# Token weight kept in its own column order, first keys and queries transposed apart, third transposes moved two steps forward

## The chip, the cores and the metric

The kernel runs on one core of a Trainium2 chip. The metric is device time in microseconds (us) of one execution, lower is better. Where a difference is small, kernels are compared within rounds on one chip. The engines have short names: PE is TensorE (matmuls), PEld its weight loads, ACT is ScalarE, DVE is VectorE, POOL is GpSimd. SBUF and PSUM are the two memories in which the kernel keeps its tiles; its matmuls write to PSUM. A *span* is the length that the trace covers; it is about 1.8 us less than the time (374.2 against 376.01 in the kernel before).

## The reference

A squared-ReLU attention without softmax feeds a two-stage mixer: first a product over tokens with a residual, then a product over channels with a residual.

```python
# q, k, v: 8 x 12 x 448 x 64, float32
scores = q @ k.T / sqrt(64)
attn   = maximum(scores, 0)**2 / 448
x      = heads_joined(attn @ v)                       # 8 x 448 x 768
h      = maximum(x.T @ w_tok1, 0) @ w_tok2            # tokens 448 -> 256 -> 448
u      = x + h.T
out    = u + maximum(u @ w_ch1, 0) @ w_ch2            # channels 768 -> 1536 -> 768
```

## The kernel before

Work goes in *groups* of four heads: 24 groups, of which three make one batch entry. Each group takes seven *steps*; a step makes the scores of 64 keys on PE, the ReLU on ACT, the square on DVE, and later the product with the values on PE. The mixer's products of earlier groups are put between the steps. The order on each engine is that of the program; nothing is rescheduled.

The kernel divides its PSUM into slots: two slots `att` (scores), one each of `acc0` and `acc1`, and two slots `bank`. A tile that takes a slot waits until the last tile there has been read: in the trace of the kernel before, PE stood 0.49 us ahead of the first token matmuls, until DVE had copied `qkT` out of the `bank` slots.

Tokens are loaded as `(p c)`, token = 7p + c, so that every load is contiguous. Inside the kernel tokens are kept as `(c p)`. The second token weight, whose columns are tokens, therefore has to be put into `(c p)` order: GpSimd does that with two copies.

```python
def load_wt2():
    nc.gpsimd.dma_start(out=wt2_nat, in_=moe_w_tok2.rearrange("(c j) s -> j c s", c=JC))

def order_wt2():
    for j in range(JC):                                   # JC = 2
        nc.gpsimd.tensor_copy(
            wt2[:, j, :].rearrange("n (c p) -> n c p", c=QC),
            wt2_nat[:, j, :].rearrange("n (p c) -> n c p", c=QC))

def transposes(i, place="acc", split=False):
    # ... 56 transposing matmuls: queries and keys of group i into two PSUM slots
    for r in range(2):                                    # then one copy of each, 128x896
        (nc.scalar.copy if split and r == 0 else nc.vector.tensor_copy)(
            sb[:, r].rearrange("n w t -> n (w t)"), parts[r][:, : 2 * S])

def x_back(i, place="bank", copy=None):
    # ... 8 transposing matmuls into a tile x_ps in `place`, then one copy to x_sb

def token2(i, ...):
    # ... h_ps = r1^T @ wt2, two matmuls for each r
        nc.vector.tensor_tensor(                          # the residual addition
            out=uT_tiles[b // 2][:, 2 * d + r, off : off + S],
            in0=parts[r][:, :S], in1=xT[b % 2][:, 2 * d + r, :S], op=ALU.add)
```

The opening, before PE's queue is full of mixer work, is written out by hand. Its `keep_clock` matmuls of zeros were put there with the intent of keeping PE's clock up.

```python
load_four(0, "kqv"); load_four(1, "qk"); load_wt1(); load_four(2, "qk")
load_four(1, "v");   load_wt2();         load_four(2, "v"); load_four(3, "qk")
order_wt2()
load_wc1(0, 2);      load_four(3, "v")
keep_clock(2, warm_ps)                       # matmuls of zeros
transposes(0, "acc", split=True)
keep_clock(3, warm_ps)
for i in range(DB):                          # groups 0, 1, 2
    for c in range(QC):                      # 7 steps
        scores(i, c, alone=(i, c) == (0, 2))
        if i == 0:
            keep_clock(0 if c in (3, 4) else 1 if c > 4 else 2, warm_ps)
        # ...
        square(keep=1)
        # ... values of group i-1 at c < 3, token2(i-2) at c = 1, 2
        if c == 4 and i > 0:
            x_back(i - 1, place="acc0", copy=nc.scalar.copy if i > 1 else None)
        if c == 5 and i > 0:
            transposes(i + 1, "bank")
        if c == 6:
            values(i, (0, 1))                # opens acc0 and acc1
            if i > 0:
                token1(i - 1)                # the first token matmuls
```

## Time and profile before

| | us |
|---|---|
| time, median of 3 | 376.94 (376.81 to 377.26) |
| PE busy, in a span of 374.2 | 365.0 |
| residual additions on DVE, 48 | 27.7 |

The prediction below shows the head of the page, the stretches and the chain. Three more lines of the timeline of the kernel before serve as marks for everything that follows (columns: start, length, engine, line, operation, tiles; in brackets the idle time before it and what ended it): the first scores, the first token matmuls, and the first use of the reordered weight.

```profile
7.74 0.38 PE L172 MATMUL sc_ps<-qkT 64*64 64x448 bf16 x4 [0.36 <-ACT qkT L162]
...
20.00 1.03 PE L276 MATMUL t_ps<-x_sb,wt 128*128 128x256 bf16 x8 [0.49 <-DVE qkT L162]
...
22.23 0.55 PE L335 MATMUL h_ps<-wt,r_sb 128*128 128x448 bf16 x2
```

From the group of residual additions (mean ns of one after the bar):

```profile
L345 DVE TENSOR_TENSOR uT_sb<-h_ps,xT 128x448 bf16<-128x448 f32 x48 | 27.7, 617 | 9.3 <-PE h_ps L335 9.3
```

### The profile page before, as it was taken

The page shows a single profiled execution, that of the slowest core. Times are in us where ns is not written, and L with a number is a line of the kernel's source. Part 1 is how long each engine was busy: PE and PEld are TensorE (multiplying, and loading weights), DVE is VectorE, ACT ScalarE, POOL GpSimd, SP SyncE. Part 2 cuts the span into 40 slices and gives each one's busy share as a digit, 9 for nine tenths or more (in the row PEclk, how much of TensorE's full clock was granted, in tenths as well). Part 3 has the DMA queues.
Part 4 walks back from the last instruction along what each step waited for, and adds up shares of the span by engine and source line. Part 5 has one row for each costly group of instructions (what it writes and reads, how often), then busy time and mean ns, then how long its engine had stood idle before and what let it go on. Part 6 is the DMA issues. An engine that isn't in the chain of part 4 may idle for free.

```text
span 374.2 us, 10241 instructions
## 1 busy us (share of the span) xinstructions
PE 365.0 (98%) x4379; PEld 201.8 (54%) x4379; DVE 213.1 (57%) x413; ACT 211.5 (57%) x313; POOL 101.2 (27%) x187
## 2 busy tenths in 40 slices
PE   8889999999999999999999999999999999999996
PEld 3544555455555555565555555555555654555554
DVE  2996688756576666475555684575555755131022
ACT  4987888776345368725765457752775456312400
POOL 8975448304221403430330303412310000000000
PEclk9999999999999999999999999999999999999999
DMA  8999999923997876766755677757560434233024
GB/s 153 126 141 202 181 206 185 170 44 66 141 169 166 168 133 99 114 108 151 108 92 92 112 142 132 111 77 159 112 95 13 99 81 98 58 70 86 0 54 116
DMA packets 69565, 43.32 MB, mean 116 GB/s; under 512 B 43472, under 2 KB 66064, under 8 KB 69520
## 3 DMA queue, kind: packets, MB, share of 16 engines
q0 software_dynamic: 24496, 21.49, 40.3%
q1 hardware_dynamic: 44640, 20.75, 25.6%
q8 instruction: 34, 0.56, 0.6%
q10 hardware_dynamic: 384, 0.43, 0.4%
q14 instruction: 11, 0.09, 0.1%
HBM read 43.42 MB, written 11.01 MB: 145 GB/s over the span
## 4 chain that ended last, share of the span: by engine, by line
PE 90%; DVE 5%; ACT 3%; issue 1%; DVEq 0%; ACTq 0%
PE m_ps L425 29%; PE m_ps L386 28%; PE sc_ps L172 9%; PE acc_ps L205 9%; PE h_ps L335 4%; PE t_ps L294 3%; PE qkT_ps L148 3%; ACT at L186 2%; DVE at L193 2%; PE t_ps L310 1%; DVE uT_sb L345 1%; PE t_ps L276 1%; PE warm_ps L521 1%; DVE qkT L162 1%; PE x_ps L258 1%
## 5 line engine op out<-in xcount | busy, mean ns | idle before, releaser
L186 ACT ACTIVATE at<-sc_ps 128x896 bf16<-128x896 f32 x167 | 144.9, 924 | 48.6 <-PE sc_ps L172 48.5
L193 DVE TENSOR_TENSOR at<-at 128x896 bf16<-128x896 bf16 x168 | 99.2, 628 | 54.5 <-ACT at L186 54.4
L386 PE MATMUL m_ps<-uT_sb,wc 128*128 128x448 bf16 x564 | 115.5, 353 | 0.2 <-DVE uT_sb L345 0.2
L425 PE MATMUL m_ps<-wc,r_sb 128*128 128x384 bf16 x660 | 113.2, 326 | 0.0
L425 PEld LDWEIGHTS <-r_sb 128*128 128x128 bf16 x660 | 62.7, 98 | 46.7 <-issue 6.1
L393 ACT ACTIVATE r_sb<-m_ps 128x448 bf16<-128x448 f32 x94 | 51.3, 546 | 56.0 <-PE m_ps L386 55.6
L386 PEld LDWEIGHTS <-wc 128*128 128x128 bf16 x564 | 52.3, 98 | 53.4 <-issue 8.3
L432 DVE TENSOR_TENSOR out_sb<-m_ps,u_sb 128x384 f32<-128x384 f32 x55 | 30.6, 556 | 48.3 <-PE m_ps L425 46.8
L172 PE MATMUL sc_ps<-qkT 64*64 64x448 bf16 x672 | 54.1, 358 | 1.0 <-ACT at L186 0.6
L223 DVE TENSOR_SCALAR xT<-acc_ps 128x448 bf16<-128x448 f32 x45 | 26.1, 620 | 27.6 <-PE acc_ps L205 27.6
L205 PE MATMUL acc_ps<-at,v_raw 64*64 64x448 bf16 x672 | 41.0, 350 | 0.8 <-ACT x_sb L267 0.5
L642 POOL COPY gate<-x_sb 1x1 bf16<-1x1 bf16 x12 | 3.1, 261 | 126.6 <-DMA x_sb<-xT 126.6
L84 POOL DMA_DIRECT2D q_raw<-in_q_dram x48 | 28.9, 613 | 18.7 <-DMA wc<-in_moe_w_ch_dram 16.3
L345 DVE TENSOR_TENSOR uT_sb<-h_ps,xT 128x448 bf16<-128x448 f32 x48 | 27.7, 617 | 9.3 <-PE h_ps L335 9.3
L84 POOL DMA_DIRECT2D v_raw<-in_v_dram x48 | 29.6, 643 | 5.9 <-DMA wc<-in_moe_w_ch_dram 4.5
L320 ACT ACTIVATE r_sb<-t_ps 128x256 bf16<-128x256 f32 x36 | 11.8, 381 | 32.5 <-PE t_ps L310 28.3
L162 DVE COPY qkT<-qkT_ps 128x896 bf16<-128x896 bf16 x45 | 26.0, 619 | 6.7 <-PE qkT_ps L148 6.7
L205 PEld LDWEIGHTS <-v_raw 64*64 64x64 bf16 x672 | 21.9, 106 | 14.6 <-issue 4.8
L172 PEld LDWEIGHTS <-qkT 64*64 64x64 bf16 x672 | 17.5, 105 | 21.7 <-issue 17.8
L84 POOL DMA_DIRECT2D k_raw<-in_k_dram x46 | 28.1, 633 | 1.7 <-issue 1.7
L335 PE MATMUL h_ps<-wt,r_sb 128*128 128x448 bf16 x96 | 22.3, 353 | 0.0
L294 PE MATMUL t_ps<-x_sb,wt 128*128 128x256 bf16 x108 | 14.7, 273 | 0.0
(53 smaller groups left out, 153.1 us busy)
## 6 DMA issues: line engine op xcount, KB each, us to landing
out_dram<-out_sb SPq DMA_DIRECT2D x54, 192.0 KB, 3.1
q_raw<-in_q_dram POOLq DMA_DIRECT2D x48, 112.0 KB, 4.0
v_raw<-in_v_dram POOLq DMA_DIRECT2D x48, 112.0 KB, 5.3
k_raw<-in_k_dram POOLq DMA_DIRECT2D x46, 112.0 KB, 4.5
wc<-in_moe_w_ch_dram POOLq DMA_DIRECT2D x4, 1152.0 KB, 10.6
u_sb<-uT_sb SPq DMA_TRANSPOSE x48, 2.6
x_sb<-xT SPq DMA_TRANSPOSE x16, 3.3
k_first<-in_k_dram SPq DMA_DIRECT2D x1, 224.0 KB, 3.5
```

The source lines that it names most:

```text
L84: eng.dma_start(out=dst[64 * r : 64 * (r + 1)].rearrange("p g c d -> p g (c d)"), in_=src[b, h0 : h0 + 2].rearrange("g (p c) d -> p g (c d ...
L162: (nc.scalar.copy if split and r == 0 else nc.vector.tensor_copy)(sb[:, r].rearrange("n w t -> n (w t)"), parts[r][:, : 2 * S])
L172: nc.tensor.matmul(ps[64 * r : 64 * (r + 1), g, :S], lhsT=sb[h, r, 1, c * 64 : (c + 1) * 64], rhs=sb[h, r, 0, :], start=True, stop=True, s ...
L186: nc.scalar.activation(at, ps[:, :, :S], AF.Relu)
L193: nc.vector.tensor_tensor(out=at, in0=at, in1=at, op=ALU.mult)
L205: nc.tensor.matmul(ps[r][64 * g : 64 * (g + 1), :S], lhsT=v_raw[h, g, c, :], rhs=at[h, g, :], start=(c == 0), stop=(c == QC - 1), skip_gro ...
L335: nc.tensor.matmul(parts[r][:, :S], lhsT=r1[:, j, r * 128 : (r + 1) * 128], rhs=wt2[:, j, :], start=(j == 0), stop=(j == JC - 1),)
L345: nc.vector.tensor_tensor(out=uT_tiles[b // 2][:, 2 * d + r, off : off + S], in0=parts[r][:, :S], in1=xT[b % 2][:, 2 * d + r, :S], op=ALU.add,
L386: nc.tensor.matmul(ps[:, :S], lhsT=wc1[:, g, e * 128 : (e + 1) * 128], rhs=uT[:, g, off : off + S], start=(g == 0), stop=(g == CC - 1),)
L393: nc.scalar.activation(r2[:, e, off : off + S], ps[:, :S], AF.Relu)
L425: nc.tensor.matmul(ps[:, :HN], lhsT=r2[:, e, t * 128 : (t + 1) * 128], rhs=wc2[:, e, cols], start=(e == 0), stop=(e == EC - 1),)
L432: nc.vector.tensor_tensor(out=o[:, cols].rearrange("n (g d) -> n g d", d=128), in0=ps[:, :HN].rearrange("n (g d) -> n g d", d=128), in1=u_ ...
```

## The change

The intent is a shorter opening: take GpSimd's copies out of the way by reading the PSUM result in permuted order instead; let the first scores start sooner; and bring the third transposes (group 2) forward, so that their copies do not stand between `x_sb` and the first token matmuls. Five parts: (1) no reordering, (2) the permuted read, (3) the first keys and queries apart, (4) one pair of clock-keeping matmuls fewer, (5) the move.

```diff
-            out=wt2_nat, in_=moe_w_tok2.rearrange("(c j) s -> j c s", c=JC)
+            out=wt2, in_=moe_w_tok2.rearrange("(c j) s -> j c s", c=JC)
-    def order_wt2(): ...                                  # and its call
+    def transposes_first():
+        keys = [ps_acc.tile([128, 1024], BF16, tag=f"acc{r}", name="kT_ps") for r in range(2)]
+        queries = ps_att.tile([128, 2, 1024], BF16, tag="att", name="qT_ps")
+        # ... 28 transposes of the keys, then
+                nc.scalar.copy(sb[:, 0, 1], keys[0][:, :S])
+                nc.vector.tensor_copy(sb[:, 1, 1], keys[1][:, :S])
+        # ... 28 transposes of the queries, then
+                nc.vector.tensor_copy(sb[:, :, 0], queries[:, :, :S])
@@ the residual addition
-                out=uT_tiles[b // 2][:, 2 * d + r, off : off + S],
-                in0=parts[r][:, :S],
-                in1=xT[b % 2][:, 2 * d + r, :S],
+                out=uT_tiles[b // 2][:, 2 * d + r, off : off + S].rearrange("n (c p) -> n c p", c=QC),
+                in0=parts[r][:, :S].rearrange("n (p c) -> n c p", c=QC),
+                in1=xT[b % 2][:, 2 * d + r, :S].rearrange("n (c p) -> n c p", c=QC),
@@ the opening
-    transposes(0, "acc", split=True)
+    transposes_first()
-                keep_clock(0 if c in (3, 4) else 1 if c > 4 else 2, warm_ps)
+                keep_clock(2 if c < 3 else c // 6, warm_ps)
-            if c == 5 and i > 0:
+            if (i, c) in ((1, 3), (2, 5)):
                 transposes(i + 1, "bank")
```

More of the change, by code (lines that the diff above doesn't have):

```diff
@@ L64 @@
     wt1_last = wpool.tile([128, 128], BF16, name="wt1_last")
-    wt2_nat = wpool.tile([128, JC, S], BF16, name="wt2_nat")
     wt2 = wpool.tile([128, JC, S], BF16, name="wt2")
@@ L105, in load_wt2 @@
         nc.gpsimd.dma_start(
-            out=wt2_nat, in_=moe_w_tok2.rearrange("(c j) s -> j c s", c=JC)
+            out=wt2, in_=moe_w_tok2.rearrange("(c j) s -> j c s", c=JC)
         )
-    def order_wt2():
-        for j in range(JC):
-            nc.gpsimd.tensor_copy(
-                wt2[:, j, :].rearrange("n (c p) -> n c p", c=QC),
-                wt2_nat[:, j, :].rearrange("n (p c) -> n c p", c=QC),
-            )
     def load_wc1(i, parts):
@@ L164, in transposes @@
             )
+    def transposes_first():
+        sb = attn.tile([128, 2, 2, S], BF16, name="qkT")
+        qkT[0] = sb
+        keys = [ps_acc.tile([128, 1024], BF16, tag=f"acc{r}", name="kT_ps") for r in range(2)]
+        queries = ps_att.tile([128, 2, 1024], BF16, tag="att", name="qT_ps")
+        for w, dst in ((1, keys), (0, [queries[:, r] for r in range(2)])):
+            for c in range(QC):
+                for r in range(2):
+                    h = slice(64 * r, 64 * (r + 1))
+                    for g in range(2):
+                        nc.tensor.matmul(
+                            dst[r][64 * g : 64 * (g + 1), c * 64 : c * 64 + 64],
+                            lhsT=raws[0, "qk"[w]][h, g, c, :],
+                            rhs=ident[h, h],
+                            is_transpose=True,
+                            start=True,
+                            stop=True,
+                            skip_group_check=True,
+                        )
+            if w:
+                nc.scalar.copy(sb[:, 0, 1], keys[0][:, :S])
+                nc.vector.tensor_copy(sb[:, 1, 1], keys[1][:, :S])
+            else:
+                nc.vector.tensor_copy(sb[:, :, 0], queries[:, :, :S])
     def scores(i, c, alone=False):
@@ L544 @@
     load_four(3, "qk")
-    order_wt2()
     load_wc1(0, 2)
```

## The prediction

> **What bounds the kernel now.** I read the head of the profile page first, then busy time by stretch, then the chain of waits, and last the timeline of the stretch that was not full.
>
> From the page (busy time by engine, then busy tenths in 40 slices of 9.36 us):
>
> ```profile
> PE 365.0 (98%) x4379; PEld 201.8 (54%) x4379; DVE 213.1 (57%) x413; ACT 211.5 (57%) x313; POOL 101.2 (27%) x187
> ...
> PE   8889999999999999999999999999999999999996
> ```
>
> TensorE is busy 98% of the span, and only the first three slices and the last fall short. The table of stretches gives PE 10.00 of 10 us in 40 to 50, 50.00 of 50 in 80 to 130, and 100.00 of 100 in 200 to 300. So from about 38 us to 370 us a shorter operation elsewhere buys nothing, and a longer one costs nothing until PE has to wait for it. The change removes no useful matmul. All it can win is PE's gaps in the first 38 us, and once that opening is shorter, the full stretch behind it moves forward by as much. The stretches of the opening (columns: window, length, busy us of PE, PEld, DVE, ACT, POOL):
>
> ```profile
> 5.00:10.00 5.00, 4.64 (x95) 2.37 (x97) 1.90 (x4) 3.19 (x4) 4.45 (x10) 1.00 1.22 176
> 10.00:15.00 5.00, 4.17 (x116) 2.85 (x117) 5.00 (x10) 4.55 (x6) 5.00 (x9) 1.00 0.79 90
> 15.00:20.00 5.00, 3.99 (x102) 2.36 (x97) 4.59 (x10) 5.00 (x7) 3.36 (x6) 1.00 1.20 176
> 20.00:25.00 5.00, 4.46 (x52) 2.01 (x51) 5.00 (x8) 3.98 (x7) 4.77 (x7) 1.00 0.70 91
> 25.00:30.00 5.00, 4.48 (x113) 2.80 (x114) 4.49 (x9) 4.41 (x7) 2.31 (x4) 1.00 1.15 206
> ```
>
> PE's gaps from 5 to 30 us are 0.36+0.83+1.01+0.54+0.52 = 3.3 us; the bound there is DVE or ACT, each in turn at 5.00 of 5.00. The chain of waits says which, and when (columns: start us, duration us, what):
>
> ```profile
> 16.81 0.82 ACT at L186
> 17.63 0.02 issue
> 17.65 0.62 DVE at L193
> 18.28 0.60 DVE x_sb L267
> 18.88 0.53 DVE at L193
> 19.41 1.07 DVE qkT L162 x2
> 20.48 2.06 DVE at L193 x2
> 22.54 0.22 issue
> 22.76 0.61 DVE at L193
> 23.37 0.55 DVE uT_sb L345
> 23.92 0.04 issue
> 23.96 0.20 ACT xT L219
> ```
>
> ACT leads up to 17.6 us, then DVE from 17.65 to 23.9, then ACT. The "20.48 2.06" step is odd: two squares in 2.06 us, where the two copies before them took 1.07.
>
> [...] The square reads `at` from SBUF twice; GpSimd's reordering of the second token weight reads SBUF. [...] Timeline of the stretch:
>
> ```profile
> 20.23 2.12 POOL L111 COPY wt<-wt_nat 128x448 bf16<-128x448 bf16 x2 [1.87 <-DMA wt_nat<-in_moe_w_tok_dram]
> 20.39 2.98 DVE L193 TENSOR_TENSOR at<-at 128x896 bf16<-128x896 bf16 x3
> ```
>
> and the squares' durations (ns min/median/max), in 20.2 to 23.5 us, then in 12.7 to 16.3:
>
> ```profile
> L193 DVE TENSOR_TENSOR at<-at x3: 611/1203/1319, 20.4 to 22.8; 128x896 bf16<-128x896 bf16 x3
> L193 DVE TENSOR_TENSOR at<-at x6: 619/622/627, 12.8 to 15.6; 128x896 bf16<-128x896 bf16 x6
> ```
>
> Two squares lost 1203+1319-2x622 = 1278 ns while the two GpSimd copies ran.
>
> [...] The kernel before has no VectorE read of PSUM at a 28-byte step, so the trace decides nothing.
>
> **The change part by part.**
>
> 1. Reordering of the second token weight removed. POOL loses two copies (880 and 1294 ns) and the 1.87 us it waited for their input. DVE gets 1.28 us back, on the chain. POOL reaches the load of half the first channel weight at about 18.4 instead of 22.3 us, which fills a hole in which the DMA engines stood at a share of 0.19 and 0.16 (22 to 24 us). Nobody waits for that load: it landed at 22.3+9.2 = 31.5 and was first used at 33.4.
>
> 2. Permuted read in 48 residual additions: the same 448 elements at 617 ns each; only the PSUM operand's inner step grows from 4 to 28 bytes. If free: 0. [...]
>
> 3. First keys and queries apart. Before, the last transpose let both copies start at 6.8; ACT's 896 elements took 0.91 us and PE's scores waited for it until 7.73. Afterwards the key copies (448 elements[...]) run beside the query transposes, and one DVE copy of 2x448 (0.62, as the old DVE copy of 896) starts at about 6.85 and ends at 7.45. Scores 0.24 us earlier. The six clock-keeping matmuls end at 7.37, so they don't hold it.
>
> 4. One clock-keeping pair fewer (at c=5 of the first group). Before, PE waited 0.67 us at 12.40 for a DVE copy because that pair needed a bank. ACT ran without a gap from 10.38 to 16.38, so this wait was just tied; removing it is what lets part 3's 0.24 us through. Alone: about 0.
>
> 5. Third transposes (group 2) two steps earlier: PE work and the two DVE copies (1.07 us) move from after the fifth score step to after the third. DVE had 0.36 us idle before 17.65; the copies start near 17.0 and use it. More important, the first token matmul waited at 20.0 for those copies to free its banks; now it needs only `x_sb`, which I place at 19.25. ACT's next result, at(2,0), comes at about 20.8 instead of 21.56. The risk is the data: the second half of those keys was issued at 12.3 and landed 4.1 us later, at 16.4, and the transposes would now ask for it at about 16.1. Estimate: PE stands 0.3 us, just covered because ACT is the bound until 17.4.
>
> Sum: the gains overlap, since parts 1 and 5 relieve the same DVE chain (17.65 to 23.4) and then ACT's own chain limits. ACT restarts at 20.3 instead of 21.07 and runs nearly gapless to 26.9, so about 0.8 us passes (0.24 of it part 3), while DVE's further relief (the first residual addition at 22.2 instead of 23.3) is partly slack. I choose 0.8 to 1.3 us, 1.0 as the middle, if the permuted read is free.
>
> **Rivals.**
>
> A. The permuted read is slow. [...] I give it 30%.
>
> B. The moved transposes wait for their keys: [...]the next scores wait too and ACT starves. For: 16.4 against 16.1. Against: only 0.3 us. If the load were 1 us later, half the gain goes: 376.5.
>
> C. The opening is held by something later anyway (data of group 4, or the channel weight's landing), so the shift is absorbed by about 37 us. Against: groups 3 and 4 were landed 2 us or more before use, and part 1 only moves loads forward. Time: 376.9.
>
> D. GpSimd's copies hid in the chain (DVE just waits for ACT instead). Partly built in above: that is why I count 1.0, not 1.9.
>
> **Range and chances.** [...]the free case is the likelier, so I name 376.1, a little above its centre of 375.9. Low 375.0: all of parts 1, 3 and 5 (1.28+0.24+0.36 = 1.9) pass. High 377.7: rival A nearly whole. A 2% change is 7.5 us, more than twice all the gaps in 5 to 30 us[...]: within 2% is all but certain.
>
> **What would show it.** Right: the residual addition stays at about 617 ns; no GpSimd copy of the weight, and no square over 0.7 us near 20 to 22 us; scores start near 7.5; the first token matmul near 19.3 with no wait for `qkT`; the steady stage still 100% PE, the whole shifted by about 1 us. Wrong: [...]PE waiting for `k_raw` near 16 us and ACT idle after it (B); the same steps up to 37 us and then a wait for a load (C). A slower clock in the opening, from the pair of clock-keepers that is gone, would be a cause that I have not counted.

Marks in the prediction, and in the expectations further down, stand for passages that were cut because no trace or run of this case shows what they say. The forecast's sum came to 376.5 us: 0.7 of the free case (376.94-1.0) and 0.3 of the case of a slow permuted read. The terms of the slow case, an extra time for each addition and what it would add on the path, are cut, and that weighing with them; the 376.1 that was named and the upper end of 377.7 were chosen with them in view. The estimate for part 3's key copies is cut too; in the trace after they took 532 ns on ACT and 391 ns on DVE.

## The result, and the profile after

Ratios here and below are the mean time of one kernel's fast runs over that of the other's fast runs of the same rounds, so not quite the ratio of the medians that are quoted; the brackets are 95% intervals.

| | median us | runs |
|---|---|---|
| before | 376.91 | 4 (376.81 to 377.26) |
| changed | 376.38 | 4 (376.01 to 376.56) |
| ratio | 0.9983 | [0.9966, 1.0] |

The times differ by 0.53 us: the same by the 2% measure, with an interval that reaches 1.0, and about two thirds of the 0.84 us that were predicted. The head of the page after, and its group of residual additions:

```profile
PE 365.0 (97%) x4377; PEld 201.2 (54%) x4377; DVE 212.1 (57%) x414; ACT 211.0 (56%) x313; POOL 99.1 (26%) x185
...
PE   7889999999999999999999999999999999999996
...
L363 DVE TENSOR_TENSOR uT_sb<-h_ps,xT 128x448 bf16<-128x448 f32 x48 | 27.7, 616 | 9.4 <-PE h_ps L353 9.3
```

The permuted addition took 616 ns, where the plain one took 617. The row of tenths differs in the first digit alone, and there PE is less busy than before, not more. The stretches of the opening after (window, length, busy us of PE, PEld, DVE, ACT, POOL, then clock, DMA share, GB/s):

```profile
5.00:10.00 5.00, 3.92 (x90) 2.14 (x87) 2.00 (x5) 2.64 (x4) 4.25 (x9) 1.00 1.17 170
...
20.00:25.00 5.00, 4.67 (x60) 1.93 (x52) 3.52 (x8) 3.88 (x7) 2.35 (x4) 1.00 1.20 195
```

The clock is 1.00 in all five stretches from 5 to 30 us. Below, *the lock* is what the prediction reads from the trace: two of DVE's squares took 1203 and 1319 ns while GpSimd's copies ran, against 622 ns for the middle one of the six squares in 12.7 to 16.3 us. By what mechanism was not shown. DVE in 20 to 25 us fell from 5.00 to 3.52, as the removal of the lock should make it, yet PE gained only 0.21 there. In 5 to 10 us PE lost 0.72. The chain of waits after (start, length, what) says why:

```profile
2.15 4.70 DMA q_raw<-in_q_dram
...
7.35 0.64 DVE qkT L182
...
8.03 0.41 PE sc_ps L190 x4
...
17.44 1.07 DVE qkT L154 x2
...
19.04 0.61 DVE x_sb L285
```

In this execution the first queries landed 4.70 us after their issue, at 6.84, and the first scores started at 8.03, 0.29 *later* than before. ACT, which was to restart at 20.3 (21.07 before), did so at 21.29. At the other end the copies of the third transposes (`qkT` L154) are now ahead of `x_sb`, which ends at 19.65. The timeline after, from there:

```profile
19.70 0.57 PE L223 MATMUL acc_ps<-at,v_raw 64*64 64x448 bf16 x8 [0.72 <-DVE x_sb L285]
20.20 1.05 PE L294 MATMUL t_ps<-x_sb,wt 128*128 128x256 bf16 x8
...
22.72 0.62 DVE L211 TENSOR_TENSOR at<-at 128x896 bf16<-128x896 bf16 x1 [1.48 <-ACT at L204]
```

PE no longer waits for `qkT` before the first token matmuls (second line, no bracket), as predicted. But it waits 0.72 us just ahead of them (first line). And DVE, freed of the lock, stands 1.48 us for ACT (third line). The first residual addition, predicted at 22.2, came at 23.27; before it came at 23.30. One more time is close: the second token weight, issued at 14.56, landed 7.8 us later, at about 22.4, and PE used it from 22.44. The change takes the copies away, not the dependence on when that load lands.

Measured from the first scores, the first token matmuls came after 12.26 us before and 12.17 us after. So two questions are open: where the 0.53 us come from, if the opening is hardly shorter in these two traces, and why the move brought nothing. The second has a candidate in the first line above. For the first, a single pair of traces is not enough: the profiled execution of the kernel before took 376.01 us, well under its median.

### The profile page after: what moved, and what is told of

Same layout as the page of the kernel before. It is cut to its first block, busy times and chain, and to the rows that moved or that the text cites. A ratio compares the mean times of both kernels' runs of the same rounds, so it can differ in the third digit from the quotient of the medians.

```text
span 374.7 us, 10236 instructions
## 1 busy us (share of the span) xinstructions
PE 365.0 (97%) x4377; PEld 201.2 (54%) x4377; DVE 212.1 (57%) x414; ACT 211.0 (56%) x313; POOL 99.1 (26%) x185
## 4 chain that ended last, share of the span: by engine, by line
PE 89%; DVE 6%; ACT 1%; DMA 1%; issue 1%; POOL 0%; ACTq 0%; POOLq 0%; DVEq 0%
PE m_ps L443 29%; PE m_ps L404 28%; PE acc_ps L223 9%; PE sc_ps L190 9%; PE h_ps L353 4%; PE t_ps L312 3%; DVE at L211 2%; PE qkT_ps L140 2%; PE t_ps L294 1%; DMA q_raw<-in_q_dram 1%; DVE uT_sb L363 1%; PE t_ps L328 1%; ACT at L204 1%; DVE qkT L154 1%; PE x_ps L276 1%
## 5 line engine op out<-in xcount | busy, mean ns | idle before, releaser
L211 DVE TENSOR_TENSOR at<-at 128x896 bf16<-128x896 bf16 x168 | 97.7, 619 | 55.9 <-ACT at L204 55.9
L190 PE MATMUL sc_ps<-qkT 64*64 64x448 bf16 x672 | 53.2, 358 | 1.1 <-ACT at L204 0.9
L241 DVE TENSOR_SCALAR xT<-acc_ps 128x448 bf16<-128x448 f32 x45 | 26.1, 620 | 27.6 <-PE acc_ps L223 27.6
L83 POOL DMA_DIRECT2D q_raw<-in_q_dram x48 | 28.9, 614 | 19.9 <-DMA wc<-in_moe_w_ch_dram 17.4
L223 PEld LDWEIGHTS <-v_raw 64*64 64x64 bf16 x672 | 21.4, 106 | 15.7 <-issue 5.7
L154 DVE COPY qkT<-qkT_ps 128x896 bf16<-128x896 bf16 x44 | 25.3, 616 | 5.4 <-PE qkT_ps L140 5.4
```

Of the source, the lines that this page charges most:

```text
L83: eng.dma_start(out=dst[64 * r : 64 * (r + 1)].rearrange("p g c d -> p g (c d)"), in_=src[b, h0 : h0 + 2].rearrange("g (p c) d -> p g (c d ...
L190: nc.tensor.matmul(ps[64 * r : 64 * (r + 1), g, :S], lhsT=sb[h, r, 1, c * 64 : (c + 1) * 64], rhs=sb[h, r, 0, :], start=True, stop=True, s ...
L211: nc.vector.tensor_tensor(out=at, in0=at, in1=at, op=ALU.mult)
L223: nc.tensor.matmul(ps[r][64 * g : 64 * (g + 1), :S], lhsT=v_raw[h, g, c, :], rhs=at[h, g, :], start=(c == 0), stop=(c == QC - 1), skip_gro ...
```

## The experiments

All outputs were correct. Medians, counts and ranges are of timed runs. *Opening* is the time from the first scores to the start of the fifth group's 56 transposes, both as the chain of waits of the profiled execution has them; *weight wait* is what PE waited for the reordered weight there. Kernels with the same letter ran on the same chip.

| kernel | | median us (range, runs) | ratio to before | first scores | opening | weight wait |
|---|---|---|---|---|---|---|
| before, first trace | | | | 7.74 | 30.08 | 0 |
| changed, first trace | | | | 8.03 | 29.99 | none |
| before_again | A | 376.54 (376.03 to 377.37, 5) | 0.9995 [0.9981, 1.0009] | 7.64 | 30.64 | 0.46 |
| after_again | A | 376.2 (376.01 to 377.99, 6) | 0.9991 [0.9974, 1.0008] | 7.38 | 30.96 | none |
| only_weight | A | 376.41 (375.88 to 376.51, 5) | 0.9986 [0.9972, 1.0] | 7.63 | 30.07 | none |
| xback_first | A | 376.03 (375.87 to 378.74, 6) | 0.9992 [0.997, 1.0015] | 7.67 | 30.38 | none |
| only_first | B | 376.49 (376.26 to 377.5, 6) | 0.9998 [0.9981, 1.0014] | 7.48 | 31.50 | 1.27 |
| reorder_twice | B | 378.99 (378.65 to 380.27, 6) | 1.0066 [1.0048, 1.0084] | 8.05 | 33.69 | 2.56 |
| qk2_early | B | 376.1 (375.91 to 376.29, 6) | 0.998 [0.9965, 0.9994] | 7.69 | 29.99 | none |
| qk2_early_xback | B | 375.74 (375.25 to 376.12, 6) | 0.997 [0.9956, 0.9985] | 7.62 | 29.45 | none |
| lock_kept | C | 376.48 (376.02 to 376.89, 6) | 0.9995 [0.9981, 1.0009] | 7.57 | 30.20 | none |
| weight_first | C | 375.76 (375.61 to 375.99, 5) | 0.9974 [0.9961, 0.9988] | 7.64 | 29.88 | none |
| after_third | C | 375.99 (375.77 to 376.93, 6) | 0.9984 [0.9969, 0.9998] | 7.36 | 30.10 | none |
| best_again | C | 375.47 (375.05 to 376.0, 6) | 0.9967 [0.9953, 0.998] | 7.77 | 29.46 | none |

What follows the opening, that is the span less the start of the fifth group's transposes, was 336.36 to 336.95 us in all fourteen traces, with the plain and with the permuted addition, and no kernel stands apart in it. So what is larger than this spread happens before that point, and a single trace carries a spread of some 0.3 us to either side from the rest alone. Where an effect is smaller than that, the timed runs decide, or nothing does.

**Theory and rivals, after the first comparison.** Theory: the gain comes from part 1, through the lock as predicted, and part 5 gains nothing because a new wait (the slot `acc0`) took the old one's place. Rival 1: the gain of part 1 is not the lock but the time at which the weight is ready. Rival 2: part 5 fails because the moved transposes wait for their keys. Rival 3: the gain is from part 3, and part 1 is off the path. In the expectations the lock (the 1.28 us that the squares lost) is Theory B, Rival 1 is Theory D, Rival 2 Theory C and Rival 3 Theory A; in xback_first and reorder_twice "Theory A" means the claim in its own brackets.

### The two kernels again, and the weight's parts alone

The kernel before and the changed one ran again, unedited (before_again, after_again, and later after_third). only_weight is the kernel before with parts 1 and 2 alone.

> The kernel before against itself: the noise floor. Ratio 1.000 within 0.001. In the trace, if the first queries land 0.6 us later than in the first trace, the first scores start at about 8.3 instead of 7.74 us, and the whole is longer by as much; the stretch from first scores to the first transposes after the opening stays at 30.1 us.

> The changed kernel again, timed in more rounds. Theory A (the first keys and queries apart bring nearly all of the gain, some 0.27 us, the rest is near nothing): 0.3 to 0.6 us under the kernel before. Theory B ([...]1.28 us of squares): 0.8 us or more. In the trace: residual addition 0.616 us; how late the first queries land decides when the first scores start, 7.5 us if they land by 6.3, about 8.0 if at 6.84 as in the first trace.

> The changed kernel once more, beside the others on this chip: 376.0 to 376.5 us, without a group at 377. In its trace the second token matmuls wait for no weight.

> Only the second token weight in natural order with the permuted read (no GpSimd copy); the rest as before. Theory A: no gain, 0 to 0.2 us, because ScalarE waits for the first token matmul's result at about 20 to 21 us whatever the squares cost, and is gapless after it; squares at 0.62 us, and VectorE now idles near 21 to 22.5 us for about 1 us. Theory B: 0.6 to 1.2 us faster.

In the repeated kernel before, the ratio was as expected, but its opening did not stay at 30.1 us. Over all rounds the kernel before ran 42 times, mean 376.78, spread from 375.95 to 378.11 us. Cut at 376.8, a line that was drawn after the times were seen and that no clean gap marks, 20 runs lie below (mean 376.38) and 22 above (mean 377.14). The changed kernel ran 16 times, mean 376.33, and only 2 of the 16 are above 376.8. So its mean is that of the lower part of the kernel before: the upper part is what is nearly missing. In two of the three comparisons within rounds the interval reaches or includes 1.0 (0.9983, 0.9991, 0.9984), so the size of the gain is not known well. The second trace of the kernel before (time 376.84) shows what the upper part may be:

```profile
20.43 2.47 POOL L111 COPY wt<-wt_nat 128x448 bf16<-128x448 bf16 x2 [2.17 <-DMA wt_nat<-in_moe_w_tok_dram]
...
22.95 0.35 PE L335 MATMUL h_ps<-wt,r_sb 128*128 128x448 bf16 x1 [0.46 <-POOL wt L111]
```

The weight landed 0.2 us later than in the first trace, the copies took 2.47 us instead of 2.12, and PE stood 0.46 us for the second half of the weight. The opening was 0.56 us longer.

only_weight (0.9986) has as large a gain as the changed kernel, by itself: by the ratio about 0.5 us, more than the 0.2 us at most of Theory A and less than the 0.6 us of Theory B. Its trace shows what the theory's lock is worth. The timeline, at the place of the removed wait:

```profile
22.12 0.55 PE L327 MATMUL h_ps<-wt,r_sb 128*128 128x448 bf16 x2
...
22.40 0.62 DVE L185 TENSOR_TENSOR at<-at 128x896 bf16<-128x896 bf16 x1 [0.96 <-ACT at L178]
```

DVE has its 1.28 us back and idles 0.96 us of them for ACT. The opening is 30.07 us, against 30.08 in the trace of the kernel before in which the weight was in time. In that comparison the lock was worth nothing. The kernel before shows why: the third square, at 22.76 us, needs a result that ACT began at 21.56 and took 0.91 us for, so without the lock it could have started about 0.3 us earlier at most. By the value matmuls near 27 us, which wait for ACT's copy of `x_sb`, even that is gone: they started 19.37 us after the first scores in both traces.

### The lock without the wait for the weight

lock_kept is only_weight in which GpSimd still makes the two copies, into a tile that nobody reads. The lock stays, the wait cannot occur.

```diff
+    wt2_spare = wpool.tile([128, JC, S], BF16, name="wt2_spare")
+    def order_wt2(): ...    # as before, from wt2 to wt2_spare, called at its old place
```

> The second token weight in natural order with the permuted read, as in only_weight, but GpSimd still makes its two copies, into a tile that nobody reads: [...]nobody waits for the copies. Theory D (what the reordering cost was the time from the load's landing to the second token matmul, in the runs in which the load lands late): as only_weight, 375.9 to 376.5 us in all runs, without the kernel before's group of runs at 377.0 to 377.4; squares still at 1.2 us. Theory B[...]: as the kernel before, 0.4 us or more over only_weight's 376.4.

The lock was there: the squares of the stretch (ns of the shortest, middle and longest) were

```profile
L193 DVE TENSOR_TENSOR at<-at x3: 618/978/1328, 20.2 to 22.3; 128x896 bf16<-128x896 bf16 x3
```

against 611/615/625 in only_weight: two squares were 360 and 710 ns longer than the third, beside copies of 1159 and 1283 ns. The opening was 30.20 against 30.07 us, a difference of 0.13 us, about an eighth of the 1.07 us by which these squares grew (978+1328-2x618). By the chain of waits it arises near 27.6 us, where PE waits for DVE's later copies of `qkT`. By time, lock_kept is at 0.9995 [0.9981, 1.0009] and only_weight at 0.9986 [0.9972, 1.0], on different chips: the intervals overlap, and they do not settle whether the lock has a share. None of the six runs of lock_kept was above 376.89, as Theory D said, but two were above its 376.5. Within the same rounds, all six (376.02 to 376.89) lie above all five of weight_first (375.61 to 375.99; parts 1 to 4, without the lock), 0.7 us in the mean. The two differ by parts 3 and 4 and the lock together, and their traces by only 0.32 us in the opening, so a share of the lock in the times is not excluded.

### The wait doubled

reorder_twice is the kernel before with the reordering done twice, first into a spare tile, so that the weight is surely late.

```diff
-        for j in range(JC):
+        for j, dst in [(j, dst) for dst in (wt2_spare, wt2) for j in range(JC)]:
-                wt2[:, j, :].rearrange("n (c p) -> n c p", c=QC),
+                dst[:, j, :].rearrange("n (c p) -> n c p", c=QC),
```

> The kernel before, with the GpSimd reordering done twice (first into a spare tile, then into the real one): doubles the cost that the change removes. Theory A (a delay in the opening goes through to the end whole): the second token matmuls wait until about 24.3 us instead of 22.9, and the kernel takes 1.3 to 1.9 us longer. Rival (the opening has slack, later stages absorb it): under 0.4 us longer.

It took 378.99 us, 2.4 us over the 376.63 us of the kernel before on that chip, more than was expected. The wait in the timeline, then two of the stretches (columns as above, the clock third from the end):

```profile
24.70 0.35 PE L336 MATMUL h_ps<-wt,r_sb 128*128 128x448 bf16 x1 [2.10 <-POOL wt L112]
```

```profile
23.00:24.00 1.00, 0.00 (x0) 0.00 (x0) 0.92 (x1) 0.60 (x1) 1.00 (x2) 1.00 0.13 21
...
27.00:28.00 1.00, 1.00 (x6) 0.19 (x9) 0.94 (x3) 0.97 (x2) 1.00 (x2) 0.50 0.87 38
```

PE waited 2.10 us and then 0.46 more for the weight, 2.56 in all, and the opening grew by 3.6 us, from 30.08 to 33.69. So in this execution the wait reached the end, with an addition: after PE had stood, its granted clock was 0.77 in 25 to 26 us and 0.50 to 0.52 in 26 to 29 us. Whether the addition is all from the clock was not tested apart. The profile fell on one of the two slowest runs (380.23 and 380.27); the other four took 378.65 to 379.0, some 2.0 to 2.4 us over the kernel before. They have no trace, but the rival (under 0.4 us) is refuted by all six.

### Part 3 without part 1, part 3 without part 5

only_first is the kernel before with parts 3 and 4; weight_first is the changed kernel with the third transposes at their old place (parts 1 to 4).

```diff
-            if (i, c) in ((1, 3), (2, 5)):
+            if c == 5 and i > 0:             # weight_first, against the changed kernel
```

> The kernel before with only the first keys and queries apart and one clock-keeping pair fewer. Theory A: first scores at about 7.4 us where the first queries land in time, so 0.25 us under the kernel before, less where the reordered token weight arrives late. Rival (it is held again before the first token matmul): no gain, under 0.1 us.

> The changed kernel without the move of the third transposes. Theory E (the move gives back at the x_sb copy what it wins at the banks, and asks for keys that have not landed): 375.9 to 376.3 us, the same as the changed kernel or 0.1 us better; first token matmul about 12.2 us after the first scores. Rival (the move is worth the 0.65 us of the prediction): 0.4 us or more over the changed kernel.

only_first gained nothing to speak of: 0.9998. Four of its runs are at 376.26 to 376.62, two at 377.48 and 377.5, and its profile fell on 377.48:

```profile
22.40 0.35 PE L361 MATMUL h_ps<-wt,r_sb 128*128 128x448 bf16 x1 [0.37 <-POOL wt L111]
...
23.64 0.35 PE L361 MATMUL h_ps<-wt,r_sb 128*128 128x448 bf16 x1 [0.90 <-POOL wt L111]
```

The weight landed at 21.4 us here (issued 0.4 us later than in the first trace, and 0.8 longer under way), against 20.2 there, and PE stood 0.37+0.90 = 1.27 us for it. The first scores at 7.48 us only made PE arrive sooner at a weight that landed when it did. weight_first, in which the weight needs no reordering, is the best of the partial versions: 0.9974, against 0.9986 for only_weight without part 3. The two were on different chips, the intervals overlap, and in their traces the first scores start at 7.64 and 7.63 us, so a gain of part 3 is not shown.

weight_first also judges part 5. With it (after_third, same rounds) the median is 375.99, without it 375.76; openings 30.10 and 29.88. The move brought nothing, as Theory E said, and it may have cost about 0.2 us, which these runs do not resolve. It can cost more where the keys are late: after_again, whose ACT stood 0.36 us for scores behind the late transposes, has an opening of 30.96 us.

### What holds the moved transposes back

Two waits were candidates: PE's wait of 0.72 us for `acc0`, which holds `x_ps` until DVE has copied it to `x_sb`, and the moved transposes' wait for their keys. after_again shows both in one execution:

```profile
16.80 0.41 PE L140 MATMUL qkT_ps<-ident,k_raw 64*64 64x64 bf16 x26 [0.34 <-DMA k_raw<-in_k_dram]
...
19.58 1.02 PE L223 MATMUL acc_ps<-at,v_raw 64*64 64x448 bf16 x8 [0.78 <-DVE x_sb L285]
```

xback_first makes the way to `x_sb` shorter: the transposes and the copy of `x_sb` are issued one square earlier. qk2_early makes the keys earlier: their load goes ahead of the first token weight's. qk2_early_xback does both.

```diff
+            if (i, c) == (1, 4):                  # xback_first: ahead of square(keep=1)
+                x_back(0, place="acc0")
-            if c == 4 and i > 0:
+            if c == 4 and i > 1:
@@
+    load_four(2, "qk")                            # qk2_early
     load_wt1()
-    load_four(2, "qk")
```

> The changed kernel with the copy of the first x_sb ahead of a square that nobody needs yet, in the second group. In the changed kernel the value matmuls waited 0.72 us for that copy, and the first token matmul behind them. Theory A (that wait is what spent the gain of moving the third transposes): first token matmul about 0.5 us earlier after the first scores, ScalarE's gap of 1.12 us about halved, time 0.4 to 0.6 us under the changed kernel. Rival (the opening is held by something later): under 0.15 us.

> The changed kernel with the loads of the third group's queries and keys issued ahead of the seven small loads of the first token weight. In two of three traces of the changed schedule the moved transposes waited for those keys (they landed at 16.8 and 17.4 us) and ScalarE then stood 0.36 and 0.68 us. Theory C (arrival of loads holds the moved transposes): keys land near 13 us, that gap of ScalarE is gone, first token matmul 0.2 to 0.4 us earlier after the first scores, time 0.2 to 0.5 us under the changed kernel. Rival (the copies on VectorE are the bound there): no change, under 0.15 us.

> The same with the copy of the first x_sb also ahead of the square. Theory C: the two waits of the second group are both gone; first token matmul at about 19.2 us, or 11.7 us after the first scores instead of 12.2 to 13.1; time 0.6 to 1.0 us under the changed kernel. Rival (value rows of group 1 or the second token weight arrive too late and hold the same place): under 0.3 us.

> The changed kernel with the third group's loads ahead and the x_sb copy ahead, again, to compare with the changed kernel of the same rounds: 0.3 to 0.6 us under it, and 0.9 to 1.3 us under the kernel before.

Each alone did nothing that these runs can show, against the 0.2 to 0.6 us that were expected: 376.03 and 376.1 us, openings 30.38 and 29.99. (qk2_early had no changed kernel in its rounds.) In xback_first the wait for `acc0` fell to 0.25 us, but the keys landed only at 17.4 us, and ACT then stood 0.68 us; in qk2_early no wait for the keys is left, but that for `acc0` is still 0.72. (The slowest run of xback_first, 378.74 us, was at a clock of 0.995.) With both, the first token matmuls come earlier. The timeline of qk2_early_xback:

```profile
18.75 0.57 PE L223 MATMUL acc_ps<-at,v_raw 64*64 64x448 bf16 x8 [0.19 <-DVE x_sb L285]
19.26 1.05 PE L294 MATMUL t_ps<-x_sb,wt 128*128 128x256 bf16 x8
```

The wait for `acc0` fell from 0.72 to 0.19, the first token matmuls came 11.64 us after the first scores instead of 12.17, and the opening is 29.45 us. best_again repeats the kernel: again 11.64, opening 29.46. Its ratio is 0.9967 and that of the changed kernel in the same rounds 0.9984, so it is 0.9967/0.9984 = 0.9983 of the changed kernel's time, about 0.6 us less. The two kernels' 12 runs are all within 375.05 to 376.12. This is the fastest version found; it beats both kernels.

What the move itself is worth, once both waits are shortened, is read against weight_first, which does not move the transposes:

```profile
19.72 1.03 PE L294 MATMUL t_ps<-x_sb,wt 128*128 128x256 bf16 x8 [0.49 <-DVE qkT L154]
```

There the first token matmuls came 12.08 us after the first scores, 0.44 later than in best_again, and the opening is 0.42 longer. By time, in the same rounds, the medians are 375.76 and 375.47 and the ratios 0.9974 and 0.9967: about 0.3 us, with intervals that overlap. Whether the earlier load or the earlier `x_sb` gains anything without the move was not tested.

## Why the prediction was right or wrong

The time, 376.38, is within 0.3 us of the predicted 376.1 and inside the range, and "within 2%" was right. The steps fared unequally.

- **What bounds the kernel: right.** What follows the opening took the same time in every kernel to within 0.6 us; the large effects are all in the first 38 us.
- **Part 2, the permuted read: right that it is free.** The step in the PSUM operand grew from 4 to 28 bytes, and the addition took 616 ns against 617. Rival A, given 30%, is refuted; no run showed the extra time that it put on each addition.
- **Part 1: the sign was right, the mechanism not as far as the traces show.** The step that failed is "DVE gets 1.28 us back, on the chain". DVE got them and then waited for ACT (0.96 us in only_weight, 1.48 us after), and the opening was 30.07 against 30.08 us. ACT itself waits for PE's first token matmuls (1.02 us before, 1.12 after), which DVE's later squares do not delay. The prediction counted on ACT restarting at 20.3 us; it restarted at 21.29. Its rival D said as much and was only half believed. What part 1 does remove is a wait that the first trace does not contain, because there GpSimd's copies ended at 22.35, just in time. In the two further traces with the reordering done once (before_again and only_first) PE stood 0.46 and 1.27 us for them, and reorder_twice, made to be late, shows that such a wait reaches the end (2.56 us of it, and 2.4 us more in the median time). The means of the two kernels differ by 376.78-376.33 = 0.45 us, a size that such waits in part of the runs would give. That the slower runs without a trace had this very wait is inferred, not shown; lock_kept, which cannot have it, was not clearly faster than the kernel before; and a share of the lock in the times stays open.
- **Part 3: not shown.** The first scores started at 7.36 and 7.38 us in two of the three traces of the changed kernel, against 7.64 and 7.74 before, but these are the two earliest of all. In the nine traces with part 3 they started between 7.36 and 8.03, the middle one at 7.64; in the five without, between 7.57 and 8.05, the middle one also at 7.64. What did get shorter is the stretch from the last group of query transposes to the scores: 1.14 to 1.33 us with part 3, 1.40 to 1.45 without. In several traces those transposes started later, so that the 0.24 us did not arrive; in the changed kernel's first trace, and in best_again, they waited for the queries to land. The prediction did not count the landing of the first queries: the slower of their first two loads took 4.1 us from issue in the first trace of the kernel before and 4.7 us in that of the changed one.
- **Part 4: as predicted**, as far as it was looked at: the wait of 0.67 us at 12.40 for DVE's copy is gone, with one of 0.47 us for ACT in its place, and the clock in the opening stayed at 1.00. It was not tested alone.
- **Part 5: wrong.** The step that failed is "now it needs only `x_sb`, which I place at 19.25". Ahead of the token matmuls, in PE's order, stand the values of step 6, which need the slot `acc0`, and `x_ps` sits there until `x_sb` is copied. The copy of `x_sb` itself was pushed back by the moved copies to 19.04 to 19.65. So the wait for `qkT` (0.49 us) was replaced by one for `acc0` (0.72). Rival B came true in part: the weight loads of the transposes waited 0.17 us for the keys in the first trace, and PE itself 0.34 in after_again. Only with both waits shortened did the first token matmuls come earlier, by 0.44 us against the kernel without the move. The prediction had moved them from 20.0 to 19.3, 0.24 of it part 3's, so about 0.5 for the move: its size was right where the two waits were out of the way.
- **The sum** came out near the truth partly by luck: about 0.5 us of part 5 and the 0.24 us of part 3 did not arrive, and a gain that was not in the reckoning, probably the late weight, stood in for them.

## What to carry to other kernels

An operand that one trace showed ready just in time was a wait of 0.46 and 1.27 us in other executions here, and the load behind it took between 5.7 us (only_weight) and 7.8 us (first trace of the changed kernel) from issue: look at how close each arrival is to its use, and take several traces before pricing its removal. Time given back to an engine counted here only up to the next thing that this engine waited for (of DVE's 1.28 us, 0.96 went into waiting for ACT), so read the bracket of its next instruction before adding it to a sum. When work is moved ahead, list every slot and every load that it now reaches first; here one slot and one load each held the gain back, and mending either alone showed nothing. To price a move, compare with the same kernel without it, not with the kernel in which it had gone wrong.
